# A third block of tokens has g @ w_out formed by seven products of halves

## The chip, the core and the metric

The kernel runs on one core of one Trainium2 chip. The core has a matrix engine (TensorE, PE in the profile; its weight loads are shown apart as PEld), a vector engine (VectorE, DVE), a scalar engine (ScalarE, ACT), GpSimd (POOL) and SyncE (SP), whose queue issues nearly all DMAs of this kernel. Each engine takes its instructions in order; engines wait for each other through semaphores. On-chip memory (SBUF) has 128 partitions; matmul results land in PSUM, in banks of 128 x 512 fp32 numbers. DMAs move data between SBUF and DRAM. The metric is the time of one execution on the device in microseconds; lower is better.

## The reference

q, k and v have 8 batches, 8 heads, 576 positions and 64 dimensions. Attention is local to chunks of 64 positions, and its output, taken as 4608 tokens of 512 numbers, goes through a feed-forward layer with mish:

```python
def _attn_ref(q, k, v):
    ...
    scores = scale * np.matmul(q_c, k_c.transpose(0, 1, 2, 4, 3))
    scores = scores - np.max(scores, axis=-1, keepdims=True)
    attn = np.exp(scores)
    attn = attn / (np.sum(attn, axis=-1, keepdims=True) + 1e-09)
    out = np.matmul(attn, v_c)

def _moe_ref(x, w_in, w_out):
    h = x @ w_in                       # 4608 x 512 @ 512 x 2048
    sp = np.where(h > 20.0, h, np.log1p(np.exp(np.minimum(h, 20.0))))
    g = h * np.tanh(sp)
    return (g @ w_out).astype(np.float32)   # 2048 x 512
```

The weights come as float64 and are turned into a high and a low fp32 part on the chip.

## The kernel before, in words

**Numbers in two parts.** In every big matrix product each operand is split into a high part (a cast) and a low part (the rest), and three matmuls, low by high, high by high and high by low, are added up in PSUM. For g these are `gh` and `gl`: a cast, and a subtraction on DVE.

**Blocks of tokens.** Tokens are taken in pairs of chunks' rows, 256 tokens each, 18 pairs. Two pairs (512 tokens) are block 0, done plainly while the weights come in (`prologue`, `slot`). The other sixteen are four blocks of 1024 tokens, m = 1 to 4. While one block is computed, the attention of the next is done beside it (`a_scores`, `a_max`, `a_sub`, `a_exp`, `a_inverse`, `a_norm`, `a_transpose`, `a_copy`, `a_values`, `a_raw`), and its operands are formed by `x_step`: eleven steps for each half of a block, seven of them splits (a cast on ACT, a subtraction on DVE), four of them differences on DVE.

**Seven products in place of eight.** In all four blocks h = x @ w_in is formed by seven products of halves (Winograd's form of Strassen's scheme). w_in is handled in eight units u of 256 columns; a unit has seven products (`product`), six matmuls of 512 columns each. Their sums are put together as PSUM is emptied: ACT copies x, DVE adds (`add`), ACT applies mish. The operands of w_in, plain blocks and sums, were written to DRAM (`ops_of`) during block 1 and are loaded again, 256 KB for each product, by `load_op`, which every product calls once: the loads run ahead of their use by the number of buffers, five (`wop_p`), or eleven in later blocks (`more`).

**g @ w_out in two ways.** `BOTH_FROM = 3` divides the blocks.

- Blocks 1 and 2 have it directly. `unit(m, u)` computes one unit's seven products. The direct matmuls of w_out's rows, twelve of 512 columns for each f (16 f of 128 rows), are put into a list, `fill`, and `filled(n)` issues n of them between products, so that PE has work while ACT and DVE empty PSUM. That covers one half of the block's tokens ("a"). `phase_two(m)` does the other half ("b"): for each f `g_split` forms gh on ACT and gl on DVE, twelve matmuls are issued, and steps of the list `todo` (the next block's x steps), two for each f, are done beside them. `wo` holds w_out's two parts in SBUF, 64 KB in each partition.
- Blocks 3 and 4 have seven products there as well. `up_two(m, n)` computes two units side by side, n = 0 to 3, product by product; there are no filler matmuls. `beside(h)`, h = 2k + i after product k of unit i, places DVE and ACT work: attention steps of the next block, sums of g (`s_sums`). Then `down_all(m)` runs 56 steps, seven products by eight units, each with twelve matmuls of 256 columns and an operand of 256 KB from DRAM (`ops_out`).

**w_out's sums.** `ops_out` is filled during block 2. For each u, four steps (`T_STEPS`) build four sums in one tile of 1 MB: `t_whole` (high plus low, DVE), `t_sums` (three subtractions, DVE), `t_hi` (a cast, ACT), `t_lo` (a subtraction, DVE, and the store of the tile). `t_keep` stores three plain blocks from `wo`, 256 KB each. `BUILDS_OUT` names their places: the build of unit n in unit n + 1 of block 2, `t_keep` at the end of unit n; the last build lies in `phase_two(2)` at f = 6 to 9. The tile comes from `c_p`, a pool of one buffer, which the outputs of blocks 1 and 2 (`store`) use too. All DMAs named here go through SP's queue, in the order of the code.

**Order.** Nothing is reordered by a scheduler: within an engine instructions run as the code issues them. The memory of `zb_p`, `wo_p`, `c_p` and `ew` is given up after block 2 (`early.close()`) and taken by the pools of blocks 3 and 4, among them `z_p` with 40 tiles for g.

Of the kernel before, what the change touches and what calls it, by code (L numbers as in the profile page):

```python
# [9 lines left out]
F32 = mybir.dt.float32  # L10
F32R = mybir.dt.float32r
# [6 lines left out]
P = 128  # L18
# [5 lines left out]
def kernel(  # L24
# [27 lines left out]
    TOK = PAIRS * PTOK  # L52
# [16 lines left out]
    make_identity(nc, ident)  # L69


    early = ctx.enter_context(ExitStack())
    zb_p = early.enter_context(tc.tile_pool(name="zb", bufs=2))
    wo_p = early.enter_context(tc.tile_pool(name="wo", bufs=1))
    c_p = early.enter_context(tc.tile_pool(name="c", bufs=1))
    ew = early.enter_context(tc.tile_pool(name="ew", bufs=2))
    wo = wo_p.tile([P, NF, 2, DM], F32R, name="wo")

    ops_of = [dram.tile([P, 7, 2, 256], F32, name=f"wa_{u}") for u in range(NU)]
    ops_out = [dram.tile([P, 7, 2, 256], F32, name=f"wb_{u}") for u in range(NU)]  # L80
# [59 lines left out]
    def w_dst(n, part):  # L140
        m, f, many = order[n]
        if m == "o":
            return wo[:, f : f + many, part]
        return wi[f // 2][:, f % 2 : f % 2 + many, part].rearrange("p m k c -> p m (k c)")

    def w_hi(n):
# [53 lines left out]
        nc.sync.dma_start(out=ops_of[u][:, 3:], in_=t)  # L200


    def t_whole(u):
        t = bld["o"] = c_p.tile([P, 4, 2, 256], F32, name=f"t_{u}", tag="c")
        hi, lo = (
            wo[:, 2 * u : 2 * u + 2, n].bitcast(F32).rearrange("p f (a c) -> p f a c", a=2)
            for n in range(2)
        )
        whole = t.rearrange("p (f a) s c -> p f a s c", a=2)[:, :, :, 1]
        nc.vector.tensor_tensor(out=whole, in0=hi, in1=lo, op=ALU.add)  # L210
# [21 lines left out]
    def t_keep(u):  # L232
        for n, (f, a) in enumerate(((0, 0), (1, 0), (1, 1))):
            nc.sync.dma_start(
                out=ops_out[u][:, n],
                in_=wo[:, 2 * u + f, :, a * 256 : (a + 1) * 256].bitcast(F32),
            )


# [152 lines left out]
    def first_pair(m):  # L392
        return PAIRS + 4 * (m - 1)
# [95 lines left out]
    def down_mm(key, f, d, t, n):  # L489
        if f == 0 and n == 0:  # L490
            acc[t] = ps_o.tile([P, DM], F32, name=f"o_{key}_{t}", tag=f"o{t}")
        g, part = ((d["gl"], 0), (d["gh"], 1), (d["gh"], 0))[n]
        nc.tensor.matmul(  # L493
            acc[t],
            lhsT=g[:, t * P : (t + 1) * P],
            rhs=wo[:, f, part],
            start=(f == 0 and n == 0),
            stop=(f == NF - 1 and n == 2),
        )
# [22 lines left out]

    def store(key, pairs, t, cuts=1):
        half, c = divmod(t, 2)
        if c == 0:
            if key == "0":
                held["o"] = raw_p.tile([P, 2, DM], F32, name=f"ob_{key}_{t}", tag="r")
            elif t == 0:
                whole = c_p.tile([P, 4, DM], F32, name=f"ob_{key}", tag="c")
                held["o"], held["next"] = whole[:, 0:2], whole[:, 2:4]  # L530
            else:
                held["o"] = held["next"]
        o = held["o"][:, c]
# [210 lines left out]

    def load_op():
        n = len(wop)
        if n < len(ops):
            m, src, u, place = ops[n]
            pool = wop_p if n < few or (n - few) % (LOOK + MORE) < LOOK else more[0]
            t = pool.tile([P, 2, 256], F32R, name=f"w{n}", tag="w")  # L750
            nc.sync.dma_start(out=t.bitcast(F32), in_=src[u][:, place])
            wop.append(t)
# [34 lines left out]
            BUILDS.setdefault(place, []).append((step, n))  # L787
    BUILDS_OUT = {}
    T_STEPS = (t_whole, t_sums, t_hi, t_lo)
    for n in range(NU):  # L790
        for i, step in enumerate(T_STEPS if n < NU - 1 else ()):
            BUILDS_OUT.setdefault((n + 1, i), []).append((step, n))
        BUILDS_OUT.setdefault((n, 7), []).append((t_keep, n))

    def unit(m, u):
        late = m == 1
        j = first_pair(m + 1) + (u - late) // 2
        begins, ends = (m < QUADS and u >= late and (u - late) % 2 == n for n in range(2))
        if u % 4 == 0:
# [95 lines left out]
    def z_of(f):  # L895
        return zb[f // 8][:, f // 2 % 4, f % 2]

    def phase_two(m):
        after = m < QUADS
        p = first_pair(m)  # L900
        todo = []
        if after:
            todo = [lambda n=n: x_step(m + 1, 0, n) for n in range(len(X_STEPS))]
            todo += [lambda: a_raw(first_pair(m + 1) + 3)]
            todo += [lambda n=n: x_step(m + 1, 1, n) for n in range(len(X_STEPS))]
        for f in range(NF):
            d = {}
            if f == 0:
                filled(12)
            g_split(d, z_of(f), f"{m}b_{f}", True)  # L910
            if f == 0:
                for t in range(TOK // P):
                    filled(3)
                    store(f"{m}a", (p, p + 2), t)
            elif after or f < NF - 1:
                filled(12)
            down((m, 1), f, d)
            for _ in range(2):
                if todo:
                    todo.pop(0)()  # L920
            if m == BOTH_FROM - 1 and 0 <= f - 6 < len(T_STEPS):
                T_STEPS[f - 6](NU - 1)
            if f == 1 and m == 1:
                a_values(first_pair(m + 1) + 3)
            if f == 10 and m + 1 < QUADS:
                load_qk(first_pair(m + 2))


# [5 lines left out]
    def bank(name, tag):  # L934
        return (ps_h if tag == "h" else ps_o).tile([P, TOK], F32, name=name, tag=tag)

    def z_new(m, u, name):
        G[u, name] = z_p.tile([P, TOK], F32, name=f"{name}_{m}_{u}", tag="z")
        return G[u, name]

    def flip(m):
        return OPEN if (m - BOTH_FROM) % 2 == 0 else (OPEN[0], OPEN[2], OPEN[1])
# [7 lines left out]
    def up_two(m, n):  # L950
# [6 lines left out]
        def beside(h):  # L957
            if h in (1, 2) and n:
                s_sums(2 * n - 3 + h)
            if h in (10, 11) and n == NU // 2 - 1:  # L960
                ready.append(operand(0, h - 10))
            if not on:
                return
            if h == 1:
                a_scores(j)
                load_v(j)
            elif h == 2:
                a_max(j)
            elif h == 3:
                a_sub(j)  # L970
                if n < 3:
                    load_qk(j + 1, pool=(ob_p, "ob"))
            elif h == 4:
                a_exp(j)
            elif h == 6:
                a_inverse(j)
            elif h == 7:
                a_norm(j)
            elif h == 10:
                a_transpose(j)  # L980
                a_copy(j)
            elif h == 12 and n < 3:
                a_values(j)
                a_raw(j)

        for k in range(7):
            for i, u in enumerate(units):
                if k == 0:
                    x[u] = bank(f"x_{m}_{u}", xt[i])
                    z11 = z_new(m, u, "G11")  # L990
                    for name in ("G12", "G21", "G22", "S1"):
                        z_new(m, u, name)
# [143 lines left out]
    with tc.manual_schedule():  # L1136
        with tc.tile_pool(name="ps_f", bufs=1, space=bass.MemoryType.PSUM) as ps_f:
            prologue(ps_f)
        ps_o = ctx.enter_context(tc.tile_pool(name="ps_o", bufs=1, space=bass.MemoryType.PSUM))
        for s in range(NF):  # L1140
            slot(s)
        for m in range(1, BOTH_FROM):
            for u in range(NU):
                unit(m, u)
            phase_two(m)
        by_token()
        p = first_pair(BOTH_FROM - 1)
        key = f"{BOTH_FROM - 1}b"
        for t in range(TOK // P):
            filled(3)  # L1150
            store(key, (p + 1, p + 3), t)
        early.close()
        more.append(ctx.enter_context(tc.tile_pool(name="wop2", bufs=MORE)))
        z_p = ctx.enter_context(tc.tile_pool(name="g", bufs=5 * NU))
        ew_l = ctx.enter_context(tc.tile_pool(name="ew2", bufs=3))
        ob_p = ctx.enter_context(tc.tile_pool(name="ob", bufs=3))
        for _ in range(MORE):
            load_op()
        for m in range(BOTH_FROM, QUADS + 1):
# [41 lines left out]
```

## Time and profile before

| What | Value |
|---|---|
| Time, median of 3 runs | 855.45 us (854.3 to 857.47) |
| Time of the profiled execution | 854.58 us |
| Its span, from the first instruction to the last | 852.8 us |
| Blocks 0 and 1, to the end of block 1's matmuls | 336.6 us |
| Block 2 | 336.6 to 515.3 us |
| Block 3: paired units, then 56 steps | 515.3 to 606.5, 606.5 to 689.5 us |
| Block 4 | 689.5 to 852.8 us |
| Mean granted TensorE clock | 0.988 |
| HBM read, written | 137.36 MB, 42.99 MB |

How to read it. A row of the windows view has a stretch of time, its length, each engine's busy time with its number of instructions, the granted TensorE clock, the busy share of the sixteen DMA engines, and the rate. A row of the timeline has the start in us, the duration, engine, line, operation, out<-in by the program's tile names, shapes, and a count of like instructions merged; brackets hold idle time before it and what ended it. PE and PEld overlap, and matmuls are pipelined: 512 columns are listed with some 0.39 us each, while one follows another after 0.23. The waits view lists who waited for whom, the sum, how often, and the longest.

### The profile page before, as it was taken

To read this page: it belongs to the slowest core of one execution; us is meant where nothing else is said; L and a number is where in the kernel's file an instruction comes from. 1 tells how busy PE (TensorE), PEld (TensorE's weight loads), DVE (VectorE), ACT (ScalarE), POOL (GpSimd) and SP (SyncE) were. 2 spreads that over 40 slices of the span, in tenths; PEclk is the share of its full clock that TensorE was granted. 3 is DMA by queue.
4 is the path that set the end of the run, shared out by engine and by line. 5 is a ranking of instruction groups with operands and counts; after the bars stand their busy time and mean duration, and the time that the engine had idled before them with its cause. 6 is when DMAs were issued, how large, how long until landed. Compare 5 with 4: busy or idle time off the path is not lost.

```text
span 852.8 us, 15933 instructions
## 1 busy us (share of the span) xinstructions
PE 810.4 (95%) x6300; PEld 686.4 (80%) x6300; DVE 521.6 (61%) x765; ACT 436.1 (51%) x640; POOL 0.7 (0%) x6
## 2 busy tenths in 40 slices
PE   4878989889999999999999999999999999999997
PEld 3756867568888888788888888877899988889997
DVE  6787889655564663665764764444788723347663
ACT  4667875444443552543543534555656534444443
POOL 0000000000000000000000000000000000000000
PEclk9988999999999999999999999999999999999999
DMA  7698883877758411788886227876567777666773
GB/s 284 238 318 291 279 282 138 263 247 268 270 204 279 111 51 57 230 286 287 258 279 212 73 99 254 301 226 184 159 164 222 216 230 195 189 195 175 209 197 88
DMA packets 96441, 181.40 MB, mean 213 GB/s; under 512 B 9072, under 2 KB 29552, under 8 KB 94320
## 3 DMA queue, kind: packets, MB, share of 16 engines
q1 hardware_dynamic: 95936, 179.74, 66.4%
q8 instruction: 50, 0.82, 0.4%
q10 hardware_dynamic: 432, 0.66, 0.2%
q14 instruction: 23, 0.19, 0.1%
HBM read 137.36 MB, written 42.99 MB: 211 GB/s over the span
## 4 chain that ended last, share of the span: by engine, by line
PE 76%; DVE 10%; DMA 5%; ACT 5%; issue 2%; SPq 1%; DVEq 0%; ACTq 0%
PE x L764 17%; PE X L1063 9%; PE v L764 9%; PE Z L1063 5%; PE y L764 5%; PE av L271 2%; DMA wst<-in_w_in 2%; PE s L271 2%; PE h L461 2%; PE o L493 2%; PE pt L339 2%; DVE wc L132 1%; PE Y L1063 1%; PE o_(1, 1)_0_2761 L493 1%; PE o_(2, 1)_0_4413 L493 1%
## 5 line engine op out<-in xcount | busy, mean ns | idle before, releaser
L764 PE MATMUL x<-x_T,w 128*128 128x512 f32 x576 | 144.7, 394 | 6.4 <-ACT zb L869 3.1
L764 PEld LDWEIGHTS x<-x_T,w 128*128 128x128 f32 x576 | 106.2, 188 | 33.3 <-ACT zb L869 4.4
L1028 ACT CAST gh<-G 128x512 fp32r<-128x512 f32 x96 | 58.8, 621 | 59.4 <-PE X L1063 32.4
L1030 DVE TENSOR_TENSOR gl<-G,gh 128x512 fp32r<-128x512 f32 x96 | 65.1, 688 | 37.3 <-ACT gh L1028 36.1
L1063 PE MATMUL X<-w,gh 128*128 128x256 f32 x512 | 72.3, 283 | 0.0
L1063 PEld LDWEIGHTS X<-w,gh 128*128 128x128 f32 x512 | 66.3, 192 | 0.2
L474 ACT ACTIVATE G<-G 128x512 f32<-128x512 f32 x48 | 30.3, 632 | 57.4 <-DVE G L776 57.4
L776 DVE TENSOR_TENSOR G<-v,G 128x512 f32<-128x512 f32 x32 | 21.9, 689 | 57.2 <-ACT G L1008 34.7
L461 PE MATMUL h<-x_first,wi 128*128 128x512 f32 (+1 forms) x204 | 49.3, 393 | 1.7 <-ACT wi L150 0.8
L764 PE MATMUL v<-x_B,w 128*128 128x512 f32 x192 | 48.8, 393 | 1.3 <-DVE zb L776 1.3
L474 ACT ACTIVATE zb<-zb 128x512 f32<-128x512 f32 x32 | 20.2, 632 | 58.0 <-DVE zb L776 58.0
L764 PE MATMUL x<-x_B,w 128*128 128x512 f32 x192 | 48.6, 394 | 0.8 <-DVE x_B L416 0.8
L764 PE MATMUL y<-x_B,w 128*128 128x512 f32 x192 | 49.1, 397 | 0.0
L764 PE MATMUL v<-x_T,w 128*128 128x512 f32 x192 | 47.6, 390 | 1.2 <-DMA w<-wa 1.2
L461 PEld LDWEIGHTS h<-x_first,wi 128*128 128x128 f32 x204 | 37.7, 195 | 10.3 <-ACT wi L150 1.2
L764 PEld LDWEIGHTS v<-x_B,w 128*128 128x128 f32 x192 | 35.5, 188 | 9.9 <-DVE zb L776 2.6
L764 PEld LDWEIGHTS v<-x_T,w 128*128 128x128 f32 x192 | 35.9, 188 | 9.3 <-issue 1.6
L1063 PE MATMUL X<-w,gl 128*128 128x256 f32 x256 | 41.8, 284 | 1.3 <-DVE gl L1030 1.2
L764 PEld LDWEIGHTS x<-x_B,w 128*128 128x128 f32 x192 | 35.2, 188 | 8.6 <-DVE x_B L416 1.2
L493 PE MATMUL o<-wo,gh 128*128 128x512 f32 x128 | 41.8, 407 | 0.3 <-DVE wo L153 0.3
L764 PEld LDWEIGHTS y<-x_B,w 128*128 128x128 f32 x192 | 35.1, 188 | 7.7
L481 DVE CAST gh<-z 128x512 fp32r<-128x512 f32 x40 | 16.9, 423 | 39.7 <-PE o_(2, 0)_3_3328 L493 20.6
(181 smaller groups left out, 1583.5 us busy)
## 6 DMA issues: line engine op xcount, KB each, us to landing
w<-wa SPq DMA_DIRECT2D x224, 256.0 KB, 3.2
w<-wb SPq DMA_DIRECT2D x112, 256.0 KB, 2.9
v<-in_v SPq DMA_DIRECT2D x16, 512.0 KB, 5.7
wa<-a SPq DMA_DIRECT2D x8, 1024.0 KB, 4.3
wb<-t SPq DMA_DIRECT2D x8, 1024.0 KB, 5.0
wst<-in_w_out SPq DMA_DIRECT2D x7, 1024.0 KB, 6.5
wst<-in_w_in SPq DMA_DIRECT2D x6, 1024.0 KB, 6.0
wa<-wi SPq DMA_DIRECT2D x24, 256.0 KB, 3.7
```

Source lines behind the costliest of these rows:

```text
L132: nc.vector.scalar_tensor_tensor(out=c, in0=x, scalar=mask, in1=y, op0=op, op1=ALU.bitwise_or)
L271: nc.tensor.matmul(o[h * CHUNK : (h + 1) * CHUNK, c, t - ts.start, g], lhsT=l[rows, t, 2 * g + h], rhs=r[rows, t, 2 * g + h], start=True, ...
L339: nc.tensor.transpose(out=d["pt", ts.start][:, t - ts.start, g], in_=d["p"][:, t, g].rearrange("p c k -> p (c k)"), identity=ident,)
L461: nc.tensor.matmul(h[:, cols], lhsT=wi[i // 2][:, i % 2, w_, kt], rhs=x[:, x_, kt, cols], start=(n == 0), stop=(n == 3 * NK - 1),)
L474: nc.scalar.activation(out=out_, in_=in_, func=AF.Mish)
L481: nc.vector.tensor_copy(out=d["gh"], in_=z)
L493: nc.tensor.matmul(acc[t], lhsT=g[:, t * P : (t + 1) * P], rhs=wo[:, f, part], start=(f == 0 and n == 0), stop=(f == NF - 1 and n == 2),)
L764: nc.tensor.matmul(o, lhsT=t[:, w_, kt], rhs=x[x_][:, kt], start=(start and i == 0), stop=(i == 5), skip_group_check=not start,)
L776: nc.vector.tensor_tensor(out=z, in0=o, in1=z, op=ALU.add)
L1028: nc.scalar.copy(out=d["gh"], in_=g)
L1030: nc.vector.tensor_tensor(out=d["gl"], in0=g, in1=d["gh"].bitcast(F32), op=ALU.subtract)
L1063: nc.tensor.matmul(o, lhsT=d[g][:, t * P : (t + 1) * P], rhs=w_[:, part], start=(k in (0, 1, 3) and u == 0 and t % 2 == 0 and n == 0), sto ...
```

## The change

`BOTH_FROM` becomes 2: blocks 2, 3 and 4 have seven products for g @ w_out, and only block 1 has `unit` and `phase_two`. w_out's sums must now be there before block 2's 56 steps, and are built in new places: builds 0 and 1 from the end of unit 6 of block 1 on, builds 2 to 4 in phase two of block 1 (f = 4 to 15), builds 5 to 7 in the first two passes of block 2's `up_two`. Phase two takes one or two steps of `todo` for an f in place of two, and leaves two x steps (T3, T4 of the second half) to the first pass.

Memory is arranged for it: w_out lies in two tiles, `wo_a` (ten f) and `wo_b` (six f, kept until builds 5 to 7 are done, then taken by the g tiles of units 5 to 7); the late builds use a pool of their own (`c2`, one buffer) which is closed before the third pass, where the tiles of gh and gl (`ew2`) come in. Outputs of block 1 go through tiles of `wop_p`, `ew` and `at` instead of `c_p`; operand loads of block 2 are held from unit 7 of block 1 until f = 3 of phase two.

```diff
+    BOTH_FROM = 2
+    FB = 10
+    wob_p = ctx.enter_context(tc.tile_pool(name="wob", bufs=1))
...
-    wo = wo_p.tile([P, NF, 2, DM], F32R, name="wo")
+    wo_a = wo_p.tile([P, FB, 2, DM], F32R, name="wo_a")
+    wo_b = wob_p.tile([P, NF - FB, 2, DM], F32R, name="wo_b", tag="b")
...
     def t_whole(u):
-        t = bld["o"] = c_p.tile([P, 4, 2, 256], F32, name=f"t_{u}", tag="c")
+        t = bld["o"] = (late_c or [c_p])[0].tile([P, 4, 2, 256], F32, name=f"t_{u}", tag="c")
...
     def store(key, pairs, t, cuts=1):
...
+        if key == "1a":
+            o = wop_p.tile([P, DM], F32, name=f"ob_{key}_{t}", tag="w")
+        elif key == "1b" and t < 2:
+            o = z_tile(f"ob_{key}_{t}")
+        else:
+            if c == 0:
+                pool, tag = (raw_p, "r") if key == "0" else (at, "A")
+                held["o"] = pool.tile([P, 2, DM], F32, name=f"ob_{key}_{t}", tag=tag)
+            o = held["o"][:, c]
...
     def load_op():
         n = len(wop)
-        if n < len(ops):
+        if n < len(ops) and not (n >= few and "hold" in held):
...
-    for n in range(NU):
-        for i, step in enumerate(T_STEPS if n < NU - 1 else ()):
-            BUILDS_OUT.setdefault((n + 1, i), []).append((step, n))
-        BUILDS_OUT.setdefault((n, 7), []).append((t_keep, n))
+    for n, places in enumerate(
+        (
+            ((6, 7), (7, 0), (7, 1), (7, 2)),
+            ((7, 6), (7, 7), 0, 1),
+            (4, 5, 6, 7),
+            (8, 9, 10, 11),
+            (12, 13, 14, 15),
+            ((0, 2, 0), (0, 3, 0), (0, 4, 0), (0, 5, 0)),
+            ((0, 9, 0), (0, 10, 0), (0, 11, 0), (0, 12, 0)),
+            ((1, 3, 0), (1, 4, 0), (1, 5, 0), (1, 6, 0)),
+        )
+    ):
+        for place, step in zip(places, T_STEPS):
+            BUILDS_OUT.setdefault(place, []).append((step, n))
+        BUILDS_OUT.setdefault(2 * n + 1, []).append((t_keep, n))
...
+    X_LAST = (8, 10)
...
     def phase_two(m):
...
+        todo += [lambda n=n: x_step(m + 1, 1, n) for n in range(len(X_STEPS)) if n not in X_LAST]
...
             down((m, 1), f, d)
-            for _ in range(2):
+            for _ in range(1 + f % 2):
                 if todo:
                     todo.pop(0)()
-            if m == BOTH_FROM - 1 and 0 <= f - 6 < len(T_STEPS):
-                T_STEPS[f - 6](NU - 1)
+            run(BUILDS_OUT, f)
...
+            if f == 3:
+                del held["hold"]
+                for _ in range(LOOK):
+                    load_op()
...
         def beside(h):
             if h in (1, 2) and n:
                 s_sums(2 * n - 3 + h)
+            if m == BOTH_FROM:
+                if n == 0 and h in (1, 2):
+                    x_step(m, 1, X_LAST[h - 1])
+                run(BUILDS_OUT, (n, h, 0))
...
-        z_p = ctx.enter_context(tc.tile_pool(name="g", bufs=5 * NU))
-        ew_l = ctx.enter_context(tc.tile_pool(name="ew2", bufs=3))
+        z_p = ctx.enter_context(tc.tile_pool(name="g", bufs=5 * NU - 2 * (NF - FB)))
         ob_p = ctx.enter_context(tc.tile_pool(name="ob", bufs=3))
+        c2_p = tc.tile_pool(name="c2", bufs=1)
+        late_c.append(c2_p.__enter__())
```

A place that is one number is an f of phase two; of two numbers, a unit of block 1 and its step; of three, a pass of `up_two` and its h.

More of the change, by code (lines that the diff above doesn't have):

```diff
@@ L76, with wo @@
     ew = early.enter_context(tc.tile_pool(name="ew", bufs=2))
-    wo = wo_p.tile([P, NF, 2, DM], F32R, name="wo")
+    wo_a = wo_p.tile([P, FB, 2, DM], F32R, name="wo_a")
+    wo_b = wob_p.tile([P, NF - FB, 2, DM], F32R, name="wo_b", tag="b")
+    def wo(f, many=1):
+        f, t = (f, wo_a) if f < FB else (f - FB, wo_b)
+        return t[:, f : f + many]
     ops_of = [dram.tile([P, 7, 2, 256], F32, name=f"wa_{u}") for u in range(NU)]
@@ L142, in w_dst @@
         if m == "o":
-            return wo[:, f : f + many, part]
+            return wo(f, many)[:, :, part]
         return wi[f // 2][:, f % 2 : f % 2 + many, part].rearrange("p m k c -> p m (k c)")
@@ L200, in s_lo @@
         nc.sync.dma_start(out=ops_of[u][:, 3:], in_=t)
+    late_c = []
     def t_whole(u):
-        t = bld["o"] = c_p.tile([P, 4, 2, 256], F32, name=f"t_{u}", tag="c")
+        t = bld["o"] = (late_c or [c_p])[0].tile([P, 4, 2, 256], F32, name=f"t_{u}", tag="c")
         hi, lo = (
-            wo[:, 2 * u : 2 * u + 2, n].bitcast(F32).rearrange("p f (a c) -> p f a c", a=2)
+            wo(2 * u, 2)[:, :, n].bitcast(F32).rearrange("p f (a c) -> p f a c", a=2)
             for n in range(2)
@@ L235, in t_keep @@
                 out=ops_out[u][:, n],
-                in_=wo[:, 2 * u + f, :, a * 256 : (a + 1) * 256].bitcast(F32),
+                in_=wo(2 * u + f)[:, 0, :, a * 256 : (a + 1) * 256].bitcast(F32),
             )
@@ L495, in down_mm @@
             lhsT=g[:, t * P : (t + 1) * P],
-            rhs=wo[:, f, part],
+            rhs=wo(f)[:, 0, part],
             start=(f == 0 and n == 0),
@@ L524, in store @@
         half, c = divmod(t, 2)
[L525 to L533, printed above, removed]
+        if key == "1a":
[7 more added lines that the diff above has]
+            o = held["o"][:, c]
         for n in range(cuts):
@@ L711 @@
     LOOK, MORE = 5, 6
-    BOTH_FROM = 3
     PRODUCTS = (
@@ L789 @@
     T_STEPS = (t_whole, t_sums, t_hi, t_lo)
-    for n in range(NU):
-        for i, step in enumerate(T_STEPS if n < NU - 1 else ()):
-            BUILDS_OUT.setdefault((n + 1, i), []).append((step, n))
-        BUILDS_OUT.setdefault((n, 7), []).append((t_keep, n))
+    for n, places in enumerate(
+        (
[8 rows of a table added]
+        )
[3 more added lines that the diff above has]
+        BUILDS_OUT.setdefault(2 * n + 1, []).append((t_keep, n))
     def unit(m, u):
         late = m == 1
+        if u == NU - 1:
+            held["hold"] = True
         j = first_pair(m + 1) + (u - late) // 2
@@ L896, in z_of @@
         return zb[f // 8][:, f // 2 % 4, f % 2]
+    X_LAST = (8, 10)
     def phase_two(m):
-        after = m < QUADS
         p = first_pair(m)
[L901 to L905, printed above, removed]
+        nxt = first_pair(m + 1)
+        todo = [lambda n=n: x_step(m + 1, 0, n) for n in range(len(X_STEPS))]
+        todo += [lambda: a_raw(nxt + 3)]
+        todo += [lambda n=n: x_step(m + 1, 1, n) for n in range(len(X_STEPS)) if n not in X_LAST]
         for f in range(NF):
@@ L914, in phase_two @@
                     store(f"{m}a", (p, p + 2), t)
-            elif after or f < NF - 1:
+            else:
                 filled(12)
             down((m, 1), f, d)
-            for _ in range(2):
+            for _ in range(1 + f % 2):
                 if todo:
                     todo.pop(0)()
-            if m == BOTH_FROM - 1 and 0 <= f - 6 < len(T_STEPS):
-                T_STEPS[f - 6](NU - 1)
-            if f == 1 and m == 1:
-                a_values(first_pair(m + 1) + 3)
-            if f == 10 and m + 1 < QUADS:
+            run(BUILDS_OUT, f)
+            if f == 1:
+                a_values(nxt + 3)
+            if f == 3:
+                del held["hold"]
+                for _ in range(LOOK):
+                    load_op()
+            if f == 10:
                 load_qk(first_pair(m + 2))
@@ L935, in bank, with z_new @@
         return (ps_h if tag == "h" else ps_o).tile([P, TOK], F32, name=name, tag=tag)
-    def z_new(m, u, name):
-        G[u, name] = z_p.tile([P, TOK], F32, name=f"{name}_{m}_{u}", tag="z")
-        return G[u, name]
+    def z_new(m, u):
+        names = ("G11", "G12", "G21", "G22")
+        if u == FB // 2:
+            held["z"] = wob_p.tile([P, 2 * (NF - FB), TOK], F32, name=f"z_{m}", tag="b")
+        for n, name in enumerate(names):
+            if u < FB // 2:
+                G[u, name] = z_p.tile([P, TOK], F32, name=f"{name}_{m}_{u}", tag="z")
+            else:
+                G[u, name] = held["z"][:, (u - FB // 2) * 4 + n]
+        G[u, "S1"] = z_p.tile([P, TOK], F32, name=f"S1_{m}_{u}", tag="z")
     def flip(m):
@@ L989, in up_two @@
                     x[u] = bank(f"x_{m}_{u}", xt[i])
-                    z11 = z_new(m, u, "G11")
-                    for name in ("G12", "G21", "G22", "S1"):
-                        z_new(m, u, name)
+                    z_new(m, u)
                 if k == 1:
@@ L1160 @@
             for n in range(NU // 2):
+                if m == BOTH_FROM and n == 2:
+                    c2_p.__exit__(None, None, None)
+                    ew_l = ctx.enter_context(tc.tile_pool(name="ew2", bufs=3))
                 up_two(m, n)
```

## The prediction

> **What bounds the kernel now.** I read the page's busy shares first, then the windows by block, then the timeline at the joins of the blocks.
>
> ```profile
> span 852.8 us, 15933 instructions
> PE 810.4 (95%) x6300; PEld 686.4 (80%) x6300; DVE 521.6 (61%) x765; ACT 436.1 (51%) x640; POOL 0.7 (0%) x6
> core 0: us, PE busy (x) PEld busy (x) DVE busy (x) ACT busy (x) POOL busy (x), PEclk, DMA share, GB/s
> 336.60:515.30 178.70, 178.15 (x1260) 146.03 (x1252) 111.25 (x163) 82.09 (x119) 0.00 (x0) 1.00 0.67 212
> 515.30:689.50 174.20, 172.64 (x1553) 154.70 (x1552) 109.71 (x165) 97.96 (x153) 0.00 (x0) 1.00 0.73 221
> ```
>
> The reader sees TensorE at its end: block 2 (first window) leaves PE idle 0.55 us of 178.70, block 3 (second window) 1.56 of 174.20. So whatever delays a matmul adds to the span, and nothing later makes it good. VectorE's 61% is an average; what matters is when its queue holds a matmul up. I took the windows' borders from these rows:
>
> ```profile
> 328.89 0.62 ACT L479 CAST gh_1b<-zb 128x512 fp32r<-128x512 f32 x1 [2.10 <-PE o_(1, 1)_3_2773 L493]
> 331.61 0.62 ACT L479 CAST gh_1b<-zb 128x512 fp32r<-128x512 f32 x1 [2.10 <-PE o_(1, 1)_3_2773 L493]
> 510.26 0.62 ACT L479 CAST gh_2b<-zb 128x512 fp32r<-128x512 f32 x1 [2.10 <-PE o_(2, 1)_3_4425 L493]
> 515.27 2.68 PEld L764 LDWEIGHTS x<-x_B,w 128*128 128x128 f32 x12
> 682.30 1.03 PEld L1063 LDWEIGHTS X<-w,gh 128*128 128x128 f32 x8
> 683.75 1.03 PEld L1063 LDWEIGHTS X<-w,gh 128*128 128x128 f32 x8
> 689.50 2.60 PEld L764 LDWEIGHTS x<-x_B,w 128*128 128x128 f32 x12
> ```
>
> Block 3 starts at 515.27, 5.01 after the last gh of block 2; block 1's matmuls would end as long after its last gh, at 331.61 + 5.01 = 336.62 (in this kernel their last twelve lie inside block 2).
>
> **The saving.** One f of the direct g @ w_out, twelve matmuls of 512 columns, takes 331.61 - 328.89 = 2.72 us; 32 of them (16 f, two halves) 87.0 us. One step of the seven products, twelve of 256 columns, takes 683.75 - 682.30 = 1.45; 56 steps 81.2. Only 5.8 us go, though an eighth of the multiplications does: weight loads (1.03 for eight) hold the smaller matmuls back. [...] In whole blocks: block 2 lasts 515.27 - 336.62 = 178.65, block 3, which has the form that block 2 gets and the same attention work, 689.50 - 515.27 = 174.23. I take the difference, **-4.4 us**, since it has the idle time of units that run in pairs without filler matmuls. Block 2's 178.65 also hold the w_out sums, which block 3 has not; they have to go elsewhere.
>
> **Where the w_out sums go.** Eight builds, each of four steps: t_whole, t_sums (DVE), t_hi (ACT), t_lo (DVE) and then a store of 1 MB from a pool of one buffer. Rows of build 7 before, and of its store:
>
> ```profile
> 487.04 1.28 DVE L416 TENSOR_TENSOR x_B<-raw,x_B 128x512 fp32r<-128x512 f32 x2
> 488.25 1.21 DVE L210 TENSOR_TENSOR t<-wo 128x1024 f32<-128x1024 f32 x1
> 491.19 1.60 DVE L219 TENSOR_TENSOR t<-t 128x512 f32<-128x512 f32 x3
> 492.82 1.06 ACT L223 CAST t<-t 128x1024 fp32r<-128x1024 f32 x1 [0.98 <-DVE t L219]
> 496.46 1.22 DVE L227 TENSOR_TENSOR t<-t 128x1024 fp32r<-128x1024 f32 x1
> DMA to landing us min/median/max: 4.5/5.0/5.6
> DVE t L210 <- DMA out<-ob_1b: 3.5, 1, 3.5
> ```
>
> DVE instructions in a row start some 0.1 us before the last one's end (two x splits 1.28, the next 1.21 after their start), so I count 0.6 for an x step or gl, 1.13 for t_whole, 1.5 for t_sums, 1.14 for t_lo. The last row shows that t_whole does wait, at the head of DVE's queue, for a store that still reads the one buffer.
>
> Builds 0 and 1 lie in units 6 and 7 of block 1, where twelve filler matmuls (2.7 us) at a time cover a late DVE; unit steps lie several us apart, so the store is out before the next t_whole. I cost them at nothing; without the cover each step's 1.1 to 1.5 us would show.
>
> Builds 2 to 4 lie in phase two of block 1, four f each, t_lo at f = 7 and 11, the next t_whole at f = 8 and 12. DVE has about 2.5 us of work in an f of 2.72, and PE's need of gl is near:
>
> ```profile
> 329.55 0.69 DVE L483 TENSOR_TENSOR gl_1b<-zb,gh_1b 128x512 fp32r<-128x512 f32 x1 [2.03 <-ACT gh_1b L479]
> 331.41 0.39 PE L493 MATMUL o_(1, 1)_0_2761<-wo,gl_1b 128*128 128x512 f32 x1
> ```
>
> gl is ready at 330.24, its weight load would start at 331.19: a reserve of 0.95, or gl's end at gh + 2.3. From gh of f = 7 as zero: gl and one x split, t_lo ends at 3.0, its store lands 5.0 later at 8.1, t_whole(3) runs to 9.2, gl of f = 9 to 9.9. Its limit is 5.44 + 2.3 = 7.75, so PE stands some 2.0 us. The two x splits and t_sums of f = 9 then put the next gl another 0.5 past its limit. At f = 11 to 13 the same comes again with a queue that is later already (t_whole(4) 1.1 after its matmuls' turn): 2.5 and 0.5. **+5.5 us**; with landings of 4.5 and 5.6 in place of 5.0, 4 to 7. What runs beside it can't hide it: gl stands behind t_whole in DVE's queue, and PE behind gl.
>
> Builds 5 to 7 lie in the first two passes of block 2's paired units. A pass is two units side by side, their seven products in turn; ACT copies or mishes what PE leaves in x, and PE adds the next product into the same x only after that. Every pass carries the attention of one pair too (maximum, a_sub, exponential, reciprocal, a_norm, in this order), and in the code a build's step comes ahead of the attention step of the same place. Block 3's first pass shows what the steps meet:
>
> ```profile
> 521.17 0.69 DVE L776 TENSOR_TENSOR G<-y,G 128x512 f32<-128x512 f32 x1 [4.78 <-PE y L764]
> 521.78 1.21 DVE L297 TENSOR_REDUCE m<-s 128x16 f32<-128x1024 f32 x1
> 521.89 0.63 ACT L474 ACTIVATE G<-G 128x512 f32<-128x512 f32 x1 [2.89 <-DVE G L776]
> 522.91 0.68 DVE L776 TENSOR_TENSOR G<-y,G 128x512 f32<-128x512 f32 x1
> 524.75 1.28 ACT L318 ACT_TABLE_LOAD   x1
> 526.04 1.06 ACT L318 ACTIVATE p<-p 128x1024 f32<-128x1024 f32 x1
> 527.01 0.57 ACT L1006 COPY G<-x 128x512 f32<-128x512 f32 x1
> 527.70 4.25 PE L764 MATMUL x<-x_T,w 128*128 128x512 f32 x18
> 530.03 0.69 DVE L776 TENSOR_TENSOR G<-v,G 128x512 f32<-128x512 f32 x1
> 532.57 1.62 PE L764 MATMUL x<-x_T,w 128*128 128x512 f32 x6
> ```
>
> The copy at 527.01 must empty x before product 4 of the second unit, which starts 1.36 after 527.70, at 529.06: 1.5 us of reserve. In the changed block 2 stand ahead of it: on DVE, after the first add's end at 521.86, the T4 split (its ACT cast waits for the mish at 521.89; done by 523.7), t_whole(5) to 524.8, the maximum to 526.0, the second add to 526.6, t_sums(5) to 528.1, a_sub to 529.3; on ACT t_hi(5) to 529.2, the table load to 530.5, the exponential to 531.5, the copy to 532.1. PE stands 3.0 us. The reciprocal chain then ends near 534.5 in place of 530.0, so the first unit's add, its mish and the next copy of x behind it run to 536.3; product 5 of the second unit (532.57) goes at 536.4. **+3.8 us** for the pass; build 6, at places 9 to 12, comes behind product 4's adds and meets slack, the store of build 5 apart. Between 2 and 5: the lower end if ACT's wait overlaps the table load, the upper if t_whole(6) waits for build 5's store as well.
>
> ```profile
> 547.40 1.21 DVE L309 TENSOR_TENSOR p<-s,m 128x1024 f32<-128x1024 f32 x1
> 551.08 1.22 DVE L323 TENSOR_REDUCE r<-p 128x16 f32<-128x1024 f32 x1 [2.46 <-ACT p L318]
> 552.83 1.22 DVE L330 TENSOR_TENSOR p<-p,r 128x1024 f32<-128x1024 f32 x1
> 555.23 0.57 ACT L1008 COPY G<-x 128x512 f32<-128x512 f32 x1
> ```
>
> Second pass, build 7, in block 3's times: t_whole before a_sub costs nothing (the table load covers it), but t_lo waits for t_hi until 552.6 and stands ahead of the sum at 551.08, which starts at 553.7; add, mish and the copy at 555.23 follow 2.6 late, and here PE starts right behind that copy. **+2.6 us**, between 0.5 and 4.
>
> The rest I cost at nothing: output buffers of the stores (older tiles, free by then), the two halves of w_out, the held weight loads (issued at f = 3, needed 35 us later), z in w_out's place (unit 5 begins after t_whole(7)). Cover gone, a late store would cost some 2.5 us once. The moved stores pass through SP and the DMA engines:
>
> ```profile
> 515.30:538.10 22.80, 22.80 (x223) 18.67 (x222) 9.10 (x12) 13.06 (x19) 0.00 (x0) 1.00 0.98 324
> 52.00:55.00 3.00, 2.41 (x5) 1.65 (x6) 2.97 (x4) 2.97 (x3) 0.00 (x0) 0.50 1.02 404
> ```
>
> The DMA engines are full in the first pass already (share 0.98), and two stores of 1 MB come into it, with build 4's store and the last operands of t_keep just ahead. At the 404 GB/s of the second row, the highest that I found, 1 MB is 2.6 us, as an estimate. PE lives in that time on eleven operands loaded in advance, one used per product, and the traffic of the first pass only refills that stock; so I take nothing, and at worst the 2.6 of one store.
>
> **Sum:** -4.4 + 5.5 + 3.8 + 2.6 = +7.5. The profiled execution took 854.58, so 862.1 us (span 860.3). The median shown, 855.45, lies 0.9 above that execution, within the runs' 3.2; I leave the forecast at **862.1**, own range 857.5 to 866.
>
> **Rivals.**
> Half of it hidden (0.20): only phase two's waits show, 854.58 - 4.4 + 5.5 = 855.7, or only the passes', 856.6. For it speaks phase two of block 2, where build 7 ran at f = 6 to 9 beside two x steps per f, and PE was never idle:
>
> ```profile
> 469.30:515.30 46.00, 46.00 (x204) 37.86 (x203) 29.77 (x46) 21.28 (x36) 0.00 (x0) 1.00 0.26 78
> ```
>
> Against it: there no second t_whole followed, so nobody waited for a store.
> All absorbed, hence faster (0.12): each queue has more reserve than I read, so that no gl and no copy of x comes past its limit: 854.58 - 4.4 = 850.2. It decides where t_whole(3) starts under some 6 us after gh of f = 7 (8.1 by my count), which a landing in 3 us would give; none was under 4.5.
> Lower clock (0.13, with late weights): a long stand makes the clock fall.
>
> ```profile
> 52.31 0.77 PE L493 MATMUL o<-wo,gl 128*128 128x512 f32 x1 [4.17 <-DVE gl L483]
> ```
>
> After 4.17 us idle the clock was 0.50 in the three microseconds quoted above; at half speed these cost 1.5 us, and I count 2 with the edges. My longest stand is 3.0; two such falls give 862.1 + 4 = 866. [...]
> That the products are not what the change says I see no room for: the lists of operands fix them.
>
> **How the numbers follow.** Forecast 0.55, half hidden 0.20, absorbed 0.12, clock or weights 0.13. A measurement tells 0.5% from no change, so faster is under 851.2, slower over 859.7. Faster: the absorbed case, 0.12. Slower: 0.13 and most of the forecast, 0.47, together 0.60. The rest 0.28. The range 851.5 to 867 leaves out most of the absorbed case and some of the clock's, under 0.2.
>
> **What would show it.** Right: in phase two of block 1 t_whole waits for a DMA of t twice, 3 us each, and PE for gl near f = 9 and 13; in block 2's first pass PE waits some 3 us for the copy of x; block 2 without these lasts near 174; weights' waits are absent. Wrong: t_whole rows with no DMA wait, passes of 22.8 us, or a block 2 far from 174 plus 6.4.

## The result, and the profile after

The changed kernel takes 865.11 us (median of 4 runs, 864.23 to 868.61), beside it the kernel before 854.88 (854.2 to 857.47): ratio 1.0122, 95% interval 1.0086 to 1.0158. It is slower by some 10 us; 862.1 was forecast. The profiled execution is the longest of the four, 868.61 us. Its page:

```profile
span 866.8 us, 16807 instructions
PE 812.2 (94%) x6588; PEld 699.3 (81%) x6588; DVE 550.6 (64%) x808; ACT 459.8 (53%) x683; POOL 0.7 (0%) x6
PE 61%; DVE 17%; DMA 8%; ACT 7%; issue 4%; SPq 3%; DVEq 0%; ACTq 0%
```

The last line is the chain of work that ended last: PE's share fell (76% before) and DVE's rose from 10% to 17%. These shares do not measure the loss: the last kernel below, which is faster than the kernel before, has 62% and 17%. PE itself is hardly busier than it was (810.4 us before). The windows view by stage, borders at the first gh of phase two and at the first product of each pass (columns as before):

```profile
291.87:343.58 51.71, 48.37 (x268) 38.55 (x266) 37.25 (x55) 22.82 (x37) 0.00 (x0) 1.00 0.75 249
343.58:370.00 26.42, 23.45 (x222) 18.36 (x221) 14.13 (x19) 13.53 (x20) 0.00 (x0) 1.00 0.97 336
370.00:400.97 30.97, 26.48 (x221) 20.78 (x220) 19.39 (x27) 16.49 (x23) 0.00 (x0) 0.89 0.77 267
400.97:529.25 128.28, 127.03 (x1113) 117.74 (x1112) 88.95 (x137) 71.54 (x116) 0.00 (x0) 1.00 0.69 202
529.25:703.40 174.15, 172.54 (x1554) 154.68 (x1554) 109.72 (x165) 98.26 (x153) 0.00 (x0) 1.00 0.72 217
```

The reader finds the change's loss in the first three rows. Phase two of block 1 and the first two passes of block 2 have idle PE; the rest of block 2 (two passes and 56 steps, 128.3 us) is as long as the same part of block 3 (174.15 less the two passes of 22.6 and 23.3). The third row has a mean clock of 0.89. All the numbers of the next table but the medians are differences of starts in the timelines: phase two from its first gh to block 2's first product, a pass from its first product to the next one's. For the kernel before, phase two is 336.62 - 289.49, and the passes are block 3's.

| Kernel | phase two | pass 1 | pass 2 | pass 3 | median us |
|---|---|---|---|---|---|
| before | 47.1 | 22.6 | 23.3 | 23.3 | 854.9 |
| after, first trace | 51.9 | 26.4 | 31.0 | 23.3 | 865.1 |
| after, second trace | 51.9 | 26.4 | 29.7 | 23.3 | (863.5, one run) |

First trace against before: 4.8 + 3.8 + 7.7 - 4.4 for the block, and 2.4 that came before phase two (its first gh is at 291.87, not 289.49), together 14.3; the spans differ by 14.0. In the second trace the part before phase two was 1.4 shorter than in the kernel before, so that piece varies from run to run and isn't the change's.

**Phase two**, timeline of the changed kernel, rows of t_whole(3) and t_whole(4), the gl behind each, and PE's waits:

```profile
319.53 1.22 DVE L221 TENSOR_TENSOR t<-wo_a 128x1024 f32<-128x1024 f32 x1 [2.62 <-DMA wb<-t]
320.67 0.68 DVE L494 TENSOR_TENSOR gl_1b<-zb,gh_1b 128x512 fp32r<-128x512 f32 x1
332.99 1.23 DVE L221 TENSOR_TENSOR t<-wo_a 128x1024 f32<-128x1024 f32 x1 [2.92 <-DMA wb<-t]
334.13 0.69 DVE L494 TENSOR_TENSOR gl_1b<-zb,gh_1b 128x512 fp32r<-128x512 f32 x1
...
321.41 0.50 PE L504 MATMUL o_(1, 1)_0_2769<-wo_a,gl_1b 128*128 128x512 f32 x1 [1.05 <-DVE gl_1b L494]
324.73 0.50 PE L504 MATMUL o_(1, 1)_0_2769<-wo_b,gl_1b 128*128 128x512 f32 x1 [0.31 <-DVE gl_1b L494]
334.87 0.50 PE L504 MATMUL o_(1, 1)_0_2769<-wo_b,gl_1b 128*128 128x512 f32 x1 [1.67 <-DVE gl_1b L494]
338.19 0.50 PE L504 MATMUL o_(1, 1)_0_2769<-wo_b,gl_1b 128*128 128x512 f32 x1 [0.30 <-DVE gl_1b L494]
```

Read a row of t_whole with its bracket: DVE had nothing to do for 2.6 us but wait for the store of t, then gl came 1.14 later, and PE's first matmul with that gl waited. The bracket of a matmul counts from the end of the matmul before it; the weight loads ahead of these four, which need the same gl, waited 1.48, 0.74, 2.09 and 0.73, together 5.0 us.

**First pass**, PE's rows with a wait, and ACT's copy ahead of the second:

```profile
353.58 1.62 PE L774 MATMUL x<-x_T,w 128*128 128x512 f32 x6 [1.49 <-DMA w<-wa]
359.78 0.57 ACT L1041 COPY G<-x 128x512 f32<-128x512 f32 x1
360.40 3.03 PE L774 MATMUL x<-x_T,w 128*128 128x512 f32 x12 [1.10 <-ACT G L1041]
364.68 1.65 PE L774 MATMUL x<-x_T,w 128*128 128x512 f32 x6 [0.38 <-ACT G L1043]
```

**Second pass**, in order of time:

```profile
369.48 1.23 DVE L221 TENSOR_TENSOR t<-wo_b 128x1024 f32<-128x1024 f32 x1 [4.13 <-DMA wb<-t]
372.43 1.05 ACT L234 CAST t<-t 128x1024 fp32r<-128x1024 f32 x1 [4.53 <-DVE t L230]
373.91 0.99 ACT L371 COPY raw<-av 128x1024 f32<-128x1024 f32 x1
374.96 1.16 PE L282 MATMUL s<-k,q 64*64 64x64 f32 x64 [1.85 <-ACT raw L371]
376.05 4.61 PE L774 MATMUL y<-x_B,w 128*128 128x512 f32 x12
...
385.14 1.28 ACT L329 ACT_TABLE_LOAD   x1 [1.20 <-DVE p L320]
388.01 3.10 PE L774 MATMUL x<-x_T,w 128*128 128x512 f32 x12 [0.55 <-ACT G L1041]
393.20 1.94 PE L350 MATMUL pt<-ident,p 128*128 128x128 f32 x8 [2.09 <-DVE p L341]
394.85 2.45 PE L774 MATMUL x<-x_T,w 128*128 128x512 f32 x6
```

Here stand two things that are not in the forecast's sum. t_whole(6), in the first pass's last part, waited 4.1 us for the store of build 5; t_hi(6) waited for it on ACT, a_raw stood behind t_hi, and the scores of the next pair need the bank that a_raw empties: PE waited 1.85. And after that wait, as after the one for the normalised p (2.09), twelve products took 4.61 in place of 3.02, six 2.45 in place of 1.65. The windows view of the two stretches shows why:

```profile
376.00:381.00 5.00, 5.00 (x24) 3.94 (x16) 2.58 (x5) 1.59 (x3) 0.00 (x0) 0.66 0.98 309
393.00:398.00 5.00, 4.80 (x18) 4.17 (x19) 1.35 (x3) 3.55 (x6) 0.00 (x0) 0.66 0.82 265
```

The granted clock was 0.66 in each: 5 x 0.34, so 1.7 us of full clock were lost each time. The pass itself loses at most that, and less where PE would have waited in that time anyhow: two kernels below that differ in one fall are 1.5 us apart.

### The profile page after: what moved, and what is told of

The parts are those of the page before. It is cut to its first block, busy times and chain, and to the rows that moved or that the text cites. A ratio compares the mean times of both kernels' runs of the same rounds, so it can differ in the third digit from the quotient of the medians.

```text
span 866.8 us, 16807 instructions
## 1 busy us (share of the span) xinstructions
PE 812.2 (94%) x6588; PEld 699.3 (81%) x6588; DVE 550.6 (64%) x808; ACT 459.8 (53%) x683; POOL 0.7 (0%) x6
## 4 chain that ended last, share of the span: by engine, by line
PE 61%; DVE 17%; DMA 8%; ACT 7%; issue 4%; SPq 3%; DVEq 0%; ACTq 0%
PE X L1098 14%; PE x L774 13%; PE Z L1098 8%; PE v L774 7%; PE y L774 4%; PE Y L1098 2%; DMA wst<-in_w_in 2%; DMA wb<-t 2%; PE av L282 2%; DVE wc L141 2%; PE pt L350 2%; PE s L282 2%; DVE m L308 1%; DVE p L341 1%; PE o_(1, 0)_3_1680 L504 1%
## 5 line engine op out<-in xcount | busy, mean ns | idle before, releaser
L1098 PE MATMUL X<-w,gh 128*128 128x256 f32 x768 | 108.3, 283 | 0.0
L1098 PEld LDWEIGHTS X<-w,gh 128*128 128x128 f32 x768 | 99.4, 192 | 0.4
L1065 DVE TENSOR_TENSOR gl<-G,gh 128x512 fp32r<-128x512 f32 x90 | 61.0, 687 | 31.1 <-ACT gh L1063 30.0
L1098 PE MATMUL X<-w,gl 128*128 128x256 f32 x384 | 62.5, 284 | 1.9 <-DVE gl L1065 1.8
L1063 ACT CAST gh<-z 128x512 fp32r<-128x512 f32 x54 | 33.5, 620 | 43.8 <-PE X L1098 26.9
L1098 PEld LDWEIGHTS X<-w,gl 128*128 128x128 f32 x384 | 53.0, 192 | 2.9 <-DVE gl L1065 2.9
L1098 PE MATMUL Z<-w,gh 128*128 128x256 f32 x384 | 53.9, 283 | 0.0
L1065 DVE TENSOR_TENSOR gl<-z,gh 128x512 fp32r<-128x512 f32 x54 | 37.0, 689 | 19.9 <-ACT gh L1063 19.1
L1098 PEld LDWEIGHTS Z<-w,gh 128*128 128x128 f32 x384 | 49.5, 192 | 0.0
L774 PE MATMUL x<-x_B,w 128*128 128x512 f32 x192 | 47.5, 392 | 0.8 <-DVE x_B L427 0.8
L485 ACT ACTIVATE z<-z 128x512 f32<-128x512 f32 x35 | 22.0, 632 | 46.4 <-DVE z L786 46.4
```

Of the source, the lines that this page charges most:

```text
L485: nc.scalar.activation(out=out_, in_=in_, func=AF.Mish)
L774: nc.tensor.matmul(o, lhsT=t[:, w_, kt], rhs=x[x_][:, kt], start=(start and i == 0), stop=(i == 5), skip_group_check=not start,)
L1063: nc.scalar.copy(out=d["gh"], in_=g)
L1065: nc.vector.tensor_tensor(out=d["gl"], in0=g, in1=d["gh"].bitcast(F32), op=ALU.subtract)
L1098: nc.tensor.matmul(o, lhsT=d[g][:, t * P : (t + 1) * P], rhs=w_[:, part], start=(k in (0, 1, 3) and u == 0 and t % 2 == 0 and n == 0), sto ...
```

## The experiments

Two theories stood against each other. The **queue theory**: PE stands because steps of the builds are ahead of urgent work in DVE's and ACT's queues, and because the one buffer makes them wait there. The **traffic theory**: the stores, more of them at once, crowd the DMA engines, whatever the order. Times with a ratio are medians; where nothing else is said the kernel before stood at 855.23 us beside them.

**Stores of phase two one f earlier.**

```diff
-            (4, 5, 6, 7),
-            (8, 9, 10, 11),
-            (12, 13, 14, 15),
+            (4, 5, 6, 6),
+            (8, 9, 10, 10),
+            (12, 13, 14, 14),
```

> Only the places of t_hi and t_lo in phase two change: t_lo of builds 2, 3, 4 stands at f = 6, 10, 14 in place of 7, 11, 15, so that each store starts one f (2.7 us) earlier and the next t_whole stays where it was. Queue theory (PE stands because t_whole, at the head of DVE's queue, waits for the one buffer's store): the waits for the DMA of t at f = 8 and 12 shrink from 2.6 and 2.9 us to under 0.8, PE's waits for gl_1b vanish, phase two from its first gh to block 2's first product goes from 51.9 to about 47.5 us, and the time falls by 4 to 5.5 us against the changed kernel (some 860 to 861). Traffic theory (the stands come from the stores' bytes sharing the DMA engines, whatever the order): the same bytes go, phase two stays at 51 to 52 and the time at 865.

Measured: phase two 49.6 us, 2.3 less; 863.13 us, ratio to before 1.0085 (1.0056 to 1.0115). t_whole(3) and (4) in the timeline of this kernel:

```profile
317.34 1.23 DVE L221 TENSOR_TENSOR t<-wo_a 128x1024 f32<-128x1024 f32 x1 [1.68 <-DMA wb<-t]
329.45 1.23 DVE L221 TENSOR_TENSOR t<-wo_a 128x1024 f32<-128x1024 f32 x1 [1.89 <-DMA wb<-t]
```

The waits shrank by one us each, not by two, since DVE now came to them earlier; PE's two long waits (1.05, 1.67) went, and three of 0.3 stayed. So the order of the stores was half of phase two's loss. The forecast of 47.5 missed the other half, most of which the last run below explains: DVE has too much to do in single f. The time, too, fell less than forecast (860 to 861), and its interval overlaps the changed kernel's; it is the rows that show the gain.

**Build 7's last steps behind the reciprocal chain.**

```diff
-            ((1, 3, 0), (1, 4, 0), (1, 5, 0), (1, 6, 0)),
+            ((1, 3, 0), (1, 4, 0), (1, 11, 0), (1, 12, 0)),
```

> Only t_hi and t_lo of build 7 move in the second paired pass, from places 5 and 6 (ahead of the reciprocal chain) to 11 and 12 (behind it). Queue theory: PE's waits for the normalised p (2.1 us) and before it for the copy of x (0.55) go, the clock does not fall after them (0.66 between 393 and 398 us in the changed kernel), and the pass goes from 31.0 to about 27 us; the time falls by some 4 us. The wait for raw ahead of the scores (1.9 us, with a fall of the clock behind it) stays. Traffic theory: the pass keeps 31 us.

Measured: second pass 25.6 us, 862.37 us, ratio 1.0077 (1.0047 to 1.0107). PE's waits of that pass are these alone, and none is for p:

```profile
373.72 1.16 PE L282 MATMUL s<-k,q 64*64 64x64 f32 x64 [1.06 <-ACT raw L371]
385.54 3.02 PE L774 MATMUL x<-x_T,w 128*128 128x512 f32 x12 [0.92 <-ACT G L1041]
389.81 1.66 PE L774 MATMUL x<-x_T,w 128*128 128x512 f32 x6 [0.38 <-ACT G L1043]
```

The wait for p went with the order alone, as the queue theory has it. The pass was 1.4 us better than expected, since the wait for raw was shorter (1.06) and no fall of the clock followed it (1.00 from 376 to 381 us, where the changed kernel has 0.66). The median fell by 2.7 us only, where 4 were forecast. The wait for the copy of x (0.92, row 385.54) did not go; in the last two kernels below, with t_whole behind a_sub, PE has no wait for this copy. The last row's wait, 0.38, stays there as well, and block 3 of the kernel before has it too (0.36, at 555.85 us).

**No DVE and ACT work, the same stores.**

```diff
+    def t_plain(u):
+        t = wo(2 * u, 2).bitcast(F32).rearrange("p f s (a c) -> p (f s) a c", a=2)
+        nc.sync.dma_start(out=ops_out[u][:, 3:], in_=t)
...
-        for place, step in zip(places, T_STEPS):
+        for place, step in zip(places, T_STEPS) if n < 2 else ((places[3], t_plain),):
```

> Builds 2 to 7 leave out t_whole, t_sums, t_hi and t_lo; in t_lo's place the same 1 MB is stored straight from w_out's two parts, so that the DMA engines carry the same bytes while DVE and ACT do none of the work (what block 2 and later multiply by is then not the sums). Queue theory: phase two about 47 us, first pass 23 to 25 (what is left is the late weights and the T4 split), second pass 23.3, time 851 to 853, under the kernel before. Traffic theory: phase two and the passes keep most of their 9 extra us, time 860 or more.

Measured: phase two 47.4, passes 23.8, 23.3, 23.3; 852.47 us, ratio 0.9963 (0.9949 to 0.9977). Phase two in the windows view:

```profile
290.71:338.07 47.36, 47.36 (x268) 39.06 (x267) 26.42 (x40) 20.11 (x34) 0.00 (x0) 1.00 0.87 295
```

PE is never idle although the DMA engines are busier (0.87) than in the changed kernel (0.75): the traffic theory falls. The loss goes with the steps; that it lies in their places and not in their work, the last two kernels show.

**t_keep's last stores earlier**, one run.

```diff
-        BUILDS_OUT.setdefault(2 * n + 1, []).append((t_keep, n))
+        BUILDS_OUT.setdefault((1, 3, 5, 7, 9, 11, 12, 13)[n], []).append((t_keep, n))
```

> The changed kernel with t_keep's last two stores (units 6, 7) at f = 12 and 13 of phase two in place of 13 and 15, so that they are out of the way of the outputs and of the first operands of block 2. Covered-wait theory (in the first pass the wait for weights, 1.5 us, lies in front of the wait for the copy of x and takes from it): the weights' wait falls under 0.5 us, PE's wait for the copy of x grows from 1.1 to about 2.5, and the pass stays at 26.0 to 26.5 us. Sum theory (each wait costs its own time): the pass falls by 1 to 1.5 us, to about 25.

Measured: first pass 26.45 us; the weights' wait is gone, and the wait for the copy of x took its time:

```profile
359.97 3.02 PE L774 MATMUL x<-x_T,w 128*128 128x512 f32 x12 [2.69 <-ACT G L1041]
```

So the late weights cost nothing of their own: the wait behind them was the longer one. That a pass has two waits doesn't mean that each can be saved. (The second pass had no wait for raw here and lasted 27.0: build 5's store landed 8.2 us after its issue, in the changed kernel 9.8. So far the traffic does matter: it sets how long a step waits at the one buffer.)

**Builds 5 and 6 left out, one at a time**, one run each. The diff is that of the kernel without steps, with `n != 5` or `n != 6` in place of `n < 2`.

> The changed kernel with the four steps of build 5 left out (first pass, places 2 to 5), the same 1 MB stored straight from w_out. By the queue theory the first pass loses t_whole, t_sums and t_hi ahead of the exponential: from 26.4 to about 24 us, what is left being the late weights and the T4 split. Build 6's t_whole then has no store of t to wait for, so the second pass loses the wait for raw (1.9) and the fall of the clock behind it (1.7): from 31.0 to about 27.5. If the wait for raw came from build 6's own length and not from the one buffer, the second pass keeps about 31.

Measured: first pass 23.9, second 27.05.

> The changed kernel with the four steps of build 6 left out (first pass, places 9 to 12), its 1 MB stored straight from w_out. Queue theory with the fall of the clock: the first pass stays at 26.4; in the second the wait for raw (1.9 us) and the 0.66 clock after it (1.7 us) go, 31.0 to about 27.4 us, while the wait for the normalised p (2.1) and the fall after that one stay. If the clock falls for another reason than PE's stand, the pass loses only 1.9 and keeps about 29.1.

Measured: first pass 26.4, second 28.5. The wait for raw is gone in both, so it hung on build 6's wait for the one buffer. Both keep the wait for p; the products behind it, from the first and from the second kernel:

```profile
387.36 1.67 PE L774 MATMUL x<-x_T,w 128*128 128x512 f32 x6 [0.58 <-ACT G L1048]
```

```profile
389.55 2.93 PE L774 MATMUL x<-x_T,w 128*128 128x512 f32 x6 [0.58 <-ACT G L1048]
```

After the same 2.10 us of standing the six products took 1.67 in one and 2.93 in the other; the granted clock of 5 us there was 1.00 in one (385.7 to 390.7) and 0.66 in the other (388 to 393). PE's waits in the pass are the same three in both kernels (copy of x 0.92, p 2.10, the next copy 0.58), so the 1.5 us between 27.05 and 28.5 are the price of the fall. Both forecasts missed a part: in the first kernel the fall after p did not come, and that 27.05 is near the 27.5 all the same is luck, since the two waits for copies grew (0.55 and none in the changed kernel's first trace). The same growth makes most of the 1.1 by which the second is over its forecast.

**The changed kernel again**, one run, to see what repeats.

> The changed kernel once more, unchanged, for a second trace of it. The waits are set by the queues and should repeat within 0.3 us: phase two 51.9, first pass 26.4, in the second pass waits of 1.9 (raw), 0.6 to 0.9 (copy of x) and 2.1 (normalised p). If the fall of the clock after a stand hangs on when the stand comes and not on its length alone, the second pass comes out anywhere from 27.6 us (no fall) to 31 (two); if the length alone decides, it is 31 again.

Measured: 51.9, 26.4 and 29.7 us; 863.48 us. The waits repeat within 0.4 us. Two of them, and the clock behind each, from the timeline and the windows view of this run:

```profile
371.00 1.16 PE L282 MATMUL s<-k,q 64*64 64x64 f32 x64 [1.76 <-ACT raw L371]
388.01 1.90 PE L350 MATMUL pt<-ident,p 128*128 128x128 f32 x8 [2.11 <-DVE p L341]
```

```profile
372.00:377.00 5.00, 5.00 (x34) 4.08 (x27) 3.80 (x6) 1.64 (x4) 0.00 (x0) 1.00 0.99 311
388.00:393.00 5.00, 4.99 (x19) 4.21 (x20) 1.16 (x2) 3.62 (x6) 0.00 (x0) 0.66 0.80 261
```

After 1.76 us no fall, after 1.85 in the first trace one. But the 2.10 us of the two kernels above came once with and once without a fall: the length alone does not decide.

**All steps moved.** One late build in each of three passes, t_whole where DVE waits for the exponential, the rest between the adds; T3 and T4 back in phase two; w_out's last rows in three tiles, so that the g of unit 5 needs only build 5 to be done before the third pass.

```diff
+            ((0, 5, 0), (0, 10, 0), (0, 11, 0), (0, 12, 0)),
+            ((1, 5, 0), (1, 10, 0), (1, 11, 0), (1, 12, 0)),
+            ((2, 5, 0), (2, 10, 0), (2, 11, 0), (2, 12, 0)),
...
+    wo_b = [wob_p.tile([P, 2, 2, DM], F32R, name=f"wo_{u}", tag=f"b{u}") for u in range(FB // 2, NU)]
...
+            held["z"] = wob_p.tile([P, 4, TOK], F32, name=f"z_{m}_{u}", tag=f"b{u}")
...
+    X_LAST = ()
```

(with the first experiment's places, and t_keep's early ones)

> All builds kept, their steps moved: phase two as in the early store, one late build in each of the first three passes with t_whole at place 5 (while DVE waits for the exponential) and t_sums, t_hi, t_lo at 10, 11, 12 (between the adds), T3 and T4 split in phase two again, t_keep's last stores at f = 11 to 13, and w_out's last six rows in three tiles so that each unit's g takes its place when its own build is done. Queue theory: phase two 47 to 48, the first three passes 22.6 to 24, 23.3 to 24 and 23.3 to 24 us, no fall of the clock in them, time 850 to 852 and so 3 to 5 us under the kernel before. Traffic theory: block 2 still lasts over 180 us and the time is 858 or more.

Measured: phase two 49.7, passes 22.6, 23.3, 23.3; 853.15 us, ratio 0.9978 (0.9959 to 0.9997). The passes are block 3's own to 0.1 us. Phase two kept 2.6 too much, and the last kernel spreads DVE's x steps over it:

```diff
-            for _ in range(1 + f % 2):
+            for _ in range((1, 1, 2, 2)[f] if f < 4 else (1, 1, 1, 3)[f % 4]):
```

> The version with all steps moved, and the x steps of phase two spread by DVE's load: one each in the f of t_whole, of t_sums and of t_lo, three in the f that has no step of a build, in place of one and two in turn. Phase two goes from 49.7 to about 47.3 us, the rest stays, so 2.3 us off: some 850.5, 4 to 5 us under the kernel before. If phase two is held by something else than DVE's load in one f (stores, weights), it stays at 49 to 50 and the time at 853.

Measured: 851.53 us beside 855.81, ratio 0.9955 (0.9940 to 0.9970): faster than the kernel before by 0.45%, clear of the noise. Windows of phase two and the three passes:

```profile
291.92:340.10 48.18, 47.85 (x269) 38.85 (x267) 38.52 (x57) 24.17 (x39) 0.00 (x0) 1.00 0.85 286
339.90:362.45 22.55, 22.55 (x222) 18.47 (x221) 12.90 (x17) 13.85 (x20) 0.00 (x0) 1.00 0.97 326
362.45:385.80 23.35, 22.98 (x222) 18.45 (x221) 15.42 (x21) 14.04 (x21) 0.00 (x0) 1.00 0.86 295
385.80:409.10 23.30, 22.91 (x221) 18.42 (x220) 15.45 (x22) 14.19 (x21) 0.00 (x0) 1.00 0.82 270
```

DVE does as much work in phase two as in the changed kernel (38.5 us beside 37.3), and PE's idle time fell from 3.3 to 0.33 us. Phase two is 48.2 us, where 47.3 was forecast: 1.5 of the 2.4 us came. DVE still waits 1.3 and 1.4 us for the store at t_whole(3) and (4), but PE is held up only once behind them, for 0.33 us.

## Why the prediction came out as it did

The direction and the mechanism were right, the size fell 3 us short: +7.5 was forecast, +10.2 lies between the medians. Of the signs named in advance the two waits for the store of t, PE's waits for gl and the 174 us came as said; that weights' waits would be absent did not.

- **The saving, -4.4:** right. In the last kernel, where nothing is in the way, block 2 takes 22.6 + 23.3 + 23.4 and 104.9 for the rest, 174.2; 174.23 was taken from block 3.
- **Builds 0 and 1 at nothing:** right. From unit 7's first product to phase two's first gh are 20.09 us in both traces (269.40 to 289.49 before, 271.78 to 291.87 after).
- **Phase two, +5.5:** measured +4.8. The four waits were put at f = 9, 10, 13 and 14 with 2.0, 0.5, 2.5 and 0.5; they are 1.48, 0.74, 2.09 and 0.73.
- **First pass, +3.8:** measured +3.8. With the weights in time (t_keep early) it came as forecast: PE waits 2.69 for the copy of x, where 3.0 was counted. In the changed kernel the weights were late by 1.5 us; they were taken at nothing with 2.6 at worst, and that this came out is luck, since they were spent out of the wait for the copy behind them.
- **Second pass, +2.6:** the step that failed; +7.7 and +6.4 in two traces. Three things were mis-sized. That build 6 "meets slack, the store of build 5 apart" left out whom ACT's queue keeps waiting: t_hi, then a_raw, then the bank of the scores, 1.8 us; the wait for the store was named, but only for the upper end of the first pass. "t_whole before a_sub costs nothing (the table load covers it)" was wrong, since the table load itself waited for a_sub (row 385.14, 1.20), which makes the copy's 0.55 to 0.92. And the fall of the clock, up to 1.7 us each time, was kept out of the sum and left to a rival. The wait for p, 2.1, was the part that was right.
- **The rivals:** half hidden and all absorbed fell by the rows of phase two and the passes. The clock's came partly true, on top of the forecast case rather than in its place. The prediction had read the fall from one stand of 4.17 us, and the longest that it counted was 3.0; these traces show falls after stands of 1.85 to 2.11. The trace of the kernel before has half the clock behind a stand shorter than 4.17 too, of 3.16 us, timeline and windows view:

```profile
115.50 1.94 PE L339 MATMUL pt<-ident,p 128*128 128x128 f32 x8 [3.16 <-DVE p L330]
115.50:118.50 3.00, 3.00 (x11) 2.73 (x12) 2.97 (x5) 2.94 (x4) 0.00 (x0) 0.50 1.01 348
```

## What to carry to other kernels

Before a step is put into an in-order queue, write down what stands behind it on that engine and how soon that is needed: here the same steps at the same DMA traffic cost 13 us in one order (865.1 beside 852.5 without them) and nothing that shows in another (851.5). With a pool of one buffer, a step that takes the buffer before the store has landed blocks its whole queue until then (t_whole(6) stood 4.13 us at the head of DVE's). And of two waits in a row, count only the later end: removing the first gave nothing (a pass of 26.45 us beside 26.4).

## What the runs showed of the hardware that was not expected

The TensorE clock fell after stands of PE well under 3 us. From phase two on, of nine stands of 1.76 to 2.7 us in six traces five were followed by slow matmuls (after 1.85 and 2.09; 2.11; 2.09; 2.10) and four were not (1.76; 2.69, 2.11; 2.10). The mean clock of the 5 us behind was 0.66 in each of the five and 1.00 in the others. Phase two of the changed kernel, where PE stood up to 1.67, has 1.00.

The two stands of 2.10 us, windows view behind them, first for the kernel without build 6, then for the one without build 5:

```profile
388.00:393.00 5.00, 4.42 (x17) 3.46 (x18) 1.05 (x2) 3.61 (x6) 0.00 (x0) 0.66 0.74 249
385.70:390.70 5.00, 4.40 (x42) 3.37 (x46) 1.41 (x3) 3.62 (x6) 0.00 (x0) 1.00 0.86 273
```

What decides between equal stands is left open: no run moved a stand on purpose.

The exponential's ACT table load was issued only when the exponential's input was there (row 385.14, after 1.20 us of waiting), so there its 1.28 us add to a late input and do not hide behind the wait. It is not so for every load: that of mish, in the first pass of the changed kernel, ran ahead of its input, and mish then waited another 1.38 us for DVE. What makes the difference is left open.

```profile
360.85 1.28 ACT L485 ACT_TABLE_LOAD   x1
363.52 0.63 ACT L485 ACTIVATE G<-G 128x512 f32<-128x512 f32 x1 [1.38 <-DVE G L786]
```
